# Transposes of Q and K straight from the loaded layout, weights loaded first, early filler matmuls, in a fused attention and FFN kernel

## The chip, the cores and the metric

The kernel runs on one core of a Trainium2 chip. The metric is the device time of one execution in microseconds (us). A kernel's executions lie within about 1% of one another. The profile is one execution taken by the hardware profiler. Its engines are PE (TensorE matmuls), PEld (weight loads), DVE (VectorE), ACT (ScalarE), POOL (GpSimd) and SP. Tiles whose names begin with ps lie in PSUM, the memory into which the matmuls of this kernel write. A column-half matmul is one of 64 columns that writes one of the two halves of the partitions.

## The reference

```python
# q, k, v: [8, 12, 448, 64] float32; attention with squared relu instead of softmax
scores = matmul(q, k^T) / sqrt(64)
attn   = maximum(scores, 0) ** 2 / 448
x      = matmul(attn, v)                    # -> [3584, 768]
xn     = x / sqrt(mean(x*x, -1) + 1e-6) * rms_g
g      = xn @ w_gate                        # [768, 1536]
out    = (g * sigmoid(g) * (xn @ w_val)) @ w_out
```

## The kernel before

The eight batches run as a software pipeline: while the PE computes the FFN of batch b (psG for gate, psV for value, psO for the output projection), units of the attention of batch b+1 and then its norm are merged between those matmuls. A head pair goes through these units: transposes (psT, copied to qkT by DVE), two score units of two row chunks each (psS), relu (three chunks on ACT, one on DVE), square (DVE), attend (psAV). The data type of the matmuls is bf16.

```python
def merge(main, side, head=0.0, tail=0.0):     # spreads side evenly over main by cost
    ...
    for c, f in main:
        while k < n and done >= total * (head + (1.0 - head - tail) * k / n):
            out.append(side[k][1]); k += 1
        out.append(f); done += c
...
ps_s = tile_pool("ps_s", bufs=2, PSUM)   # two banks each
ps_a = tile_pool("ps_a", bufs=1, PSUM)   # psT and psAV
ps_m = tile_pool("ps_m", bufs=3, PSUM)   # tag "mm": psG, psV, psO, psSS
...
# loads: q, k, v of batch 0, then
for s in range(NSL):                     # four slices of the gate and value weights
    load_w("g", s); load_w("v", s)
    if s == 1:
        alloc_ld(1); load("q", 1); load("k", 1)
load("v", 1); load_wo(0, 2); load_wo(1, 2)

def reorder(b, j):                       # DVE: put two heads side by side
    for nm in ("q", "k"):
        t = tpool.tile([PC, NCH, 2, D], BF16, ...)
        nc.vector.tensor_copy(out=t[:].rearrange("p c h d -> p h c d"),
            in_=ld[nm, b][:, 2*j : 2*j + 2, :].rearrange("p h (c d) -> p h c d", c=NCH))
        ldp[nm, b, j] = t

def transposes(b, j):
    if j == 0: ...; reorder(b, 0)
    if j + 1 < HP: reorder(b, j + 1)
    psT = ps_a.tile([P, 2, S], BF16, ...)
    for ti, nm in enumerate(("q", "k")):
        for c in range(NCH):
            nc.tensor.transpose(out=psT[:, ti, c*PC : (c+1)*PC],
                                in_=ldp[nm, b, j][:, c, :, :], identity=ident[:])
    ...nc.vector.tensor_copy(out=t[:], in_=psT[:])

def scores(b, j, cs):
    ...                                  # matmuls into psS
    for c, psS in zip(cs, pss):
        if on_dve: nc.vector.tensor_relu(out=r[:], in_=psS[:, :, :S])    # every fourth
        else:      nc.scalar.activation(out=r[:], in_=psS[:, :, :S], func=ACT.Relu)
        nc.vector.tensor_tensor(out=r[:], in0=r[:], in1=r[:], op=ALU.mult)

def attend(b, j):                        # two column halves of the array, 112 x 64 each
    for c in range(NCH):
        for hh in range(2):
            nc.tensor.matmul(out=psAV[hh*D : (hh+1)*D, :],
                lhsT=ld["v", b][:, 2*j + hh, c*D : (c+1)*D], rhs=rsq[b, j, c][:, hh, :], ...)
    ...
def norm(b):                             # psSS on PE, sqrt on ACT, reciprocal and six xn on DVE
    ...
for b in range(B):
    side = attention(b + 1) + [(1.1, lambda b=b: norm(b + 1))]
    ...                                  # issue the loads of batch b + 2
    for fn in merge(ffn(b), side, 0.0, 0.1): fn()
```

## Time and profile before

| | before |
|---|---|
| median of the runs beside the changed kernel | 548.75 us |
| span of the profile | 544.9 us |
| first psG starts | 51.6 us |
| idle time on the PE's timeline after that | 31 us |

The page of the kernel before: its busy table, then three rows of the span in 40 slices (tenths; PEclk is the granted clock of the PE).

```profile
PE 485.1 (89%) x3024; PEld 236.1 (43%) x3024; DVE 338.6 (62%) x586; ACT 252.3 (46%) x369; POOL 34.4 (6%) x45
...
PE   3774999879999799888999799987999899989996
...
PEclk9976999979999899999999999999999999999999
DMA  9999938150073402560054500733001200002013
```

The PE is the engine that sets the pace; only the first four slices (54 us) are far from full. The DMA engines are saturated in those and the next.

The waits of the kernel before (who waited for whom: us in total, times, longest):

```profile
DVE r L198 <- ACT r L197: 91.9, 123, 3.2
...
PE psT L163 <- DVE qp L148: 29.6, 8, 7.6
...
PE psS L182 <- ACT r L197: 7.4, 11, 1.0
PE psS L182 <- DVE r L195: 7.4, 9, 1.1
```

The PE's own waits are the last three lines. Where the first comes from is seen in the timeline of the kernel before, at the boundary between batches 2 and 3 (start us, duration us, engine, line, operation, out<-in, count, idle time before it and what ended it):

```profile
237.75 5.37 PE L286 MATMUL psO<-wo_sb,hT 128*128 128x256 bf16 x36
...
239.06 2.95 DVE L246 RECIPROCAL rstd<-rstd 128x448 f32<-128x448 f32 x1 [1.55 <-ACT rstd L243]
...
242.05 3.67 DVE L249 SCALAR_TENSOR_TENSOR xn<-xT,g_sb,rstd 128x448 bf16<-128x448 bf16 x6
...
245.63 0.29 DVE L148 COPY qp<-qb 112x512 bf16<-112x512 bf16 x1
...
245.97 0.37 PE L163 MATMUL psT<-ident,qp 112*128 112x112 bf16 x4 [2.85 <-DVE qp L148]
...
246.38 1.30 PE L260 MATMUL psG<-xn,wg_sb 128*128 128x448 bf16 x6
```

The output projection ends at 243.1 us. The PE's next instruction is a transpose of batch 4; it reads a reorder copy, which stands on DVE behind the reciprocal and six xn operations. psG waits behind the transposes, although its first xn slice is done before 243 us.

The second kind of wait, in the same batch. The DVE relu frees a psS buffer:

```profile
254.71 0.63 DVE L198 TENSOR_TENSOR r<-r 112x896 bf16<-112x896 bf16 x1 [1.38 <-ACT r L197]
254.93 0.40 PE L182 MATMUL psS<-qkT 64*112 64x448 bf16 x2
255.25 1.09 DVE L195 TENSOR_SCALAR r<-psS 112x896 bf16<-112x896 f32 x1
...
256.39 0.40 PE L182 MATMUL psS<-qkT 64*112 64x448 bf16 x2 [1.07 <-DVE r L195]
```

DVE idles 1.38 us for an ACT relu, because the square of that chunk stands first; only then comes the relu (255.25) for which the PE waits 1.07 us.

A group of eight transposes, and the matmul after it:

```profile
250.41 0.36 PE L163 MATMUL psT<-ident,qp 112*128 112x112 bf16 x4
...
250.61 0.36 PE L163 MATMUL psT<-ident,kp 112*128 112x112 bf16 x4
...
250.81 1.30 PE L260 MATMUL psV<-xn,wv_sb 128*128 128x448 bf16 x6
```

From start of the group to the next matmul it takes 0.40 us.

### The profile page before, as it was taken

What the parts mean: (1) busy time and instruction counts of PE and PEld (TensorE: products, weight loads), DVE (VectorE), ACT (ScalarE), POOL (GpSimd) and SP (SyncE); (2) the same over time, 40 slices, a digit from 0 to 9 for tenths busy, and PEclk for the clock granted to TensorE, in tenths of its full rate; (3) what the DMA queues carried; (4) which work ended last, traced back from release to release, by engine and by line L of the source; (5) the groups of instructions that cost most, each with busy time, mean ns of one, the idle gap of its engine ahead of it and who ended that gap; (6) DMA issues with size and microseconds to landing.
All of it is one profiled execution on the core that took longest, in us unless ns stands there. A gap on an engine that the chain in (4) does not pass through costs nothing.

```text
span 544.9 us, 7394 instructions
## 1 busy us (share of the span) xinstructions
PE 485.1 (89%) x3024; PEld 236.1 (43%) x3024; DVE 338.6 (62%) x586; ACT 252.3 (46%) x369; POOL 34.4 (6%) x45
## 2 busy tenths in 40 slices
PE   3774999879999799888999799987999899989996
PEld 1331444434444344444444444444445444444553
DVE  3886677467764677566774677656775677745210
ACT  2553454524545354535444454454545445553221
POOL 7330001000010001000010000100000000000000
PEclk9976999979999899999999999999999999999999
DMA  9999938150073402560054500733001200002013
GB/s 114 201 201 205 203 53 102 35 103 1 1 102 73 95 1 24 79 123 16 1 75 86 108 1 1 103 58 80 1 1 29 78 10 2 1 29 59 0 30 88
DMA packets 45858, 35.08 MB, mean 64 GB/s; under 512 B 2304, under 2 KB 42240, under 8 KB 45824
## 3 DMA queue, kind: packets, MB, share of 16 engines
q0 software_dynamic: 40560, 23.60, 31.7%
q1 hardware_dynamic: 5264, 11.02, 6.8%
q8 instruction: 23, 0.38, 0.3%
q14 instruction: 11, 0.09, 0.1%
HBM read 47.19 MB, written 11.01 MB: 107 GB/s over the span
## 4 chain that ended last, share of the span: by engine, by line
PE 73%; DVE 14%; ACT 8%; issue 2%; DMA 1%; POOL 0%; ACTq 0%; POOLq 0%
PE psV L260 20%; PE psG L260 20%; PE psO L286 14%; PE psAV L207 8%; PE psS L182 8%; DVE xn L249 5%; DVE rstd L246 4%; ACT r L197 4%; PE psT L163 3%; ACT L243 2%; DVE r L198 2%; DVE r L195 1%; ACT rstd L243 1%; DMA kb<-in_k_dram 1%; ACT xT L215 1%
## 5 line engine op out<-in xcount | busy, mean ns | idle before, releaser
L198 DVE TENSOR_TENSOR r<-r 112x896 bf16<-112x896 bf16 x192 | 119.3, 625 | 93.8 <-ACT r L197 91.9
L197 ACT ACTIVATE r<-psS 112x896 bf16<-112x896 f32 x144 | 127.0, 916 | 52.5 <-PE psS L182 52.4
L260 PE MATMUL psG<-xn,wg_sb 128*128 128x448 bf16 x576 | 129.4, 360 | 1.1 <-DVE xn L249 1.0
L260 PE MATMUL psV<-xn,wv_sb 128*128 128x448 bf16 x576 | 128.0, 359 | 0.0
L286 PE MATMUL psO<-wo_sb,hT 128*128 128x512 bf16 (+1 forms) x672 | 115.2, 326 | 0.0
L271 ACT ACTIVATE sil<-psG 128x448 bf16<-128x448 f32 x96 | 52.3, 545 | 102.2 <-PE psG L260 90.8
L277 DVE TENSOR_TENSOR hT<-sil,psV 128x448 bf16<-128x448 bf16 x96 | 59.4, 618 | 45.9 <-PE psV L260 37.8
L286 PEld LDWEIGHTS <-hT 128*128 128x128 bf16 x672 | 63.6, 98 | 49.2 <-issue 9.3
L182 PE MATMUL psS<-qkT 64*112 64x448 bf16 x384 | 64.5, 394 | 19.3 <-ACT r L197 7.4
L260 PEld LDWEIGHTS <-wg_sb 128*128 128x128 bf16 x576 | 53.0, 99 | 59.8 <-issue 19.2
L260 PEld LDWEIGHTS <-wv_sb 128*128 128x128 bf16 x576 | 52.3, 99 | 57.5 <-issue 19.2
L293 ACT COPY ost<-psO 128x512 f32<-128x512 f32 (+1 forms) x56 | 26.9, 480 | 81.4 <-PE psO L286 81.4
L195 DVE TENSOR_SCALAR r<-psS 112x896 bf16<-112x896 f32 x48 | 52.0, 1084 | 0.0
L207 PE MATMUL psAV<-r,vb 112*64 112x448 bf16 x384 | 47.7, 370 | 4.6 <-DVE qkT L169 3.8
L182 PEld LDWEIGHTS <-qkT 64*112 64x112 bf16 x384 | 21.1, 131 | 60.5 <-issue 55.2
L163 PE MATMUL psT<-ident,qp 112*128 112x112 bf16 x192 | 19.0, 226 | 29.6 <-DVE qp L148 29.6
L215 ACT ACTIVATE xT<-psAV 128x448 bf16<-128x448 f32 x48 | 26.1, 545 | 33.7 <-PE psAV L207 33.7
L163 PEld LDWEIGHTS <-qp 112*128 112x128 bf16 x192 | 14.0, 103 | 40.9 <-DVE qp L148 31.9
L207 PEld LDWEIGHTS <-vb 112*64 112x64 bf16 x384 | 19.1, 111 | 28.9 <-issue 21.4
L246 DVE RECIPROCAL rstd<-rstd 128x448 f32<-128x448 f32 x8 | 23.6, 2953 | 12.8 <-ACT rstd L243 12.8
L169 DVE COPY qkT<-psT 128x896 bf16<-128x896 bf16 x48 | 29.8, 620 | 2.3 <-PE psT L163 2.1
L249 DVE SCALAR_TENSOR_TENSOR xn<-xT,g_sb,rstd 128x448 bf16<-128x448 bf16 x48 | 29.3, 680 | 0.3
(39 smaller groups left out, 157.6 us busy)
## 6 DMA issues: line engine op xcount, KB each, us to landing
qb<-in_q_dram POOLq DMA_DIRECT2D x7, 672.0 KB, 7.3
kb<-in_k_dram POOLq DMA_DIRECT2D x7, 672.0 KB, 9.8
vb<-in_v_dram POOLq DMA_DIRECT2D x7, 672.0 KB, 8.1
out_dram<-ost SPq DMA_DIRECT2D x8, 336.0 KB, 2.8
wg_sb<-in_moe_w_gate_dram POOLq DMA_DIRECT2D x4, 576.0 KB, 20.2
wv_sb<-in_moe_w_val_dram POOLq DMA_DIRECT2D x4, 576.0 KB, 21.8
wo_sb<-in_moe_w_out_dram POOLq DMA_DIRECT2D x2, 1152.0 KB, 28.3
out_dram<-ost SPq DMA_DIRECT2D x8, 288.0 KB, 5.3
```

What stands on the lines that cost most here:

```text
L163: nc.tensor.transpose(out=psT[:, ti, c * PC : (c + 1) * PC], in_=ldp[nm, b, j][:, c, :, :], identity=ident[:],)
L182: nc.tensor.matmul(out=psS[:, hh, :S], lhsT=t[prt, 1, c * PC : (c + 1) * PC], rhs=t[prt, 0, :], start=True, stop=True,)
L195: nc.vector.tensor_relu(out=r[:], in_=psS[:, :, :S])
L197: nc.scalar.activation(out=r[:], in_=psS[:, :, :S], func=ACT.Relu)
L198: nc.vector.tensor_tensor(out=r[:], in0=r[:], in1=r[:], op=ALU.mult)
L207: nc.tensor.matmul(out=psAV[hh * D : (hh + 1) * D, :], lhsT=ld["v", b][:, 2 * j + hh, c * D : (c + 1) * D], rhs=rsq[b, j, c][:, hh, :], st ...
L246: nc.vector.reciprocal(out=rstd[:], in_=rstd[:])
L249: nc.vector.scalar_tensor_tensor(out=xn[:, kt, :], in0=xTs[b][:, kt, :], scalar=g_sb[:, kt : kt + 1], in1=rstd[:], op0=ALU.mult, op1=ALU.mult,
L260: nc.tensor.matmul(out=ps[:], lhsT=w_sb[:, kt, fb * P : (fb + 1) * P], rhs=xns[b][:, kt, :], start=(kt == 0), stop=(kt == KT - 1),)
L271: nc.scalar.activation(out=s[:], in_=psG[:], func=ACT.Silu)
L277: nc.vector.tensor_tensor(out=hTs[b // 2][:, fb, o : o + S], in0=sil[b, fb][:], in1=psV[:], op=ALU.mult)
L286: nc.tensor.matmul(out=ps[:, :w], lhsT=hTs[i][:, fk, t * P : (t + 1) * P], rhs=wo_sb[:, fk, o : o + w], start=(fk == 0), stop=(fk == FT - 1),)
```

## The change

The intent: transposes read the loaded tile directly (each head by itself, into one of the two partition halves of psT), so that no reorder copy is needed; all gate and value weights load before batch 1; dummy matmuls keep the PE busy in the first attention. The diff also does other things: squares are deferred to the next score unit (`pending`, `flush`), attend joins the second score unit, psT moves into the "mm" buffers, the side work spreads over 85% of the FFN instead of 90%, three relus of batch 0 move from DVE to ACT (48 to 45 on DVE), and some SBUF tiles get other buffer counts. (`transpose_dma` and the other layout in `load` are never used, since `PE_T = B`.)

```diff
     for s in range(NSL):
         load_w("g", s)
         load_w("v", s)
-        if s == 1:
-            alloc_ld(1)
-            load("q", 1)
-            load("k", 1)
-    load("v", 1)
+    for nm in ("q", "k", "v"):
+        load(nm, 1)
...
+    def keep_busy(n):
+        ps = ps_m.tile([P, S], FP32, name="psB", tag="mm")
+        for _ in range(n):
+            nc.tensor.matmul(out=ps[:], lhsT=ones_bf[:], rhs=busy_bf[:], start=True, stop=True)
...
-    def reorder(b, j):
-        ... (two DVE copies per head pair)
     def transposes(b, j):
-        psT = ps_a.tile([P, 2, S], BF16, name="psT", tag="ps_a")
+        psT = ps_m.tile([P, 2, S], BF16, name="psT", tag="mm")
         for ti, nm in enumerate(("q", "k")):
             for c in range(NCH):
-                nc.tensor.transpose(
-                    out=psT[:, ti, c * PC : (c + 1) * PC],
-                    in_=ldp[nm, b, j][:, c, :, :],
-                    identity=ident[:],
-                )
+                for hh in range(2):
+                    nc.tensor.transpose(
+                        out=psT[hh * D : (hh + 1) * D, ti, c * PC : (c + 1) * PC],
+                        in_=ld[nm, b][:, 2 * j + hh, c * D : (c + 1) * D],
+                        identity=ident[:],
+                    )
...  (in scores)
-            nc.vector.tensor_tensor(out=r[:], in0=r[:], in1=r[:], op=ALU.mult)
+            squares.append(
+                lambda r=r, eng=eng: eng.tensor_tensor(out=r[:], in0=r[:], in1=r[:], op=ALU.mult)
+            )
+        flush()
+        pending.extend(squares)
...  (in attention)
+            if b == 0:
+                add(0.3, lambda: keep_busy(2))
+            add(1.2, lambda j=j: scores(b, j, (2, 3)), lambda j=j: j and attend(b, j - 1))
+            if b == 0:
+                add(0.3, lambda: keep_busy(2))
...
+    keep_busy(16)
     for fn in merge([], attention(0) + [(1.1, lambda: norm(0))]):
...
-        for fn in merge(ffn(b), side, 0.0, 0.1):
+        for fn in merge(main, side, 0.0, 0.15):
```

More of the change, by code (lines that the diff above doesn't have):

```diff
@@ L66 @@
     ldpool = ctx.enter_context(tc.tile_pool(name="ld", bufs=2))
-    tpool = ctx.enter_context(tc.tile_pool(name="tsb", bufs=2))
+    qtpool = ctx.enter_context(tc.tile_pool(name="qkT", bufs=2))
     apool = ctx.enter_context(tc.tile_pool(name="attn", bufs=10))
-    xpool = ctx.enter_context(tc.tile_pool(name="xT", bufs=2))
+    xpool = ctx.enter_context(tc.tile_pool(name="xT", bufs=1))
     npool = ctx.enter_context(tc.tile_pool(name="norm", bufs=2))
@@ L76, with new_qkT, transpose_dma @@
     ps_m = ctx.enter_context(tc.tile_pool(name="ps_m", bufs=3, space=bass.MemoryType.PSUM))
-    def head_rows(t, b, h0, h1):
-        return t[b, h0:h1].rearrange("h (p c) d -> p h (c d)", c=NCH)
     ld = {}
-    def alloc_ld(b):
-        for nm in ("q", "k", "v"):
-            ld[nm, b] = ldpool.tile([PC, H, NCH * D], BF16, name=nm + "b", tag=nm + "b")
+    qkT = {}
+    src_of = {"q": q, "k": k, "v": v}
+    PE_T = B
     def load(nm, b, h0=0, h1=H):
-        src = {"q": q, "k": k, "v": v}[nm]
-        nc.gpsimd.dma_start(out=ld[nm, b][:, h0:h1, :], in_=head_rows(src, b, h0, h1))
+        runs = nm == "v" or b < PE_T
+        if (nm, b) not in ld:
+            shape = [PC, H, NCH * D] if runs else [PC, NCH, H * D]
+            ld[nm, b] = ldpool.tile(shape, BF16, name=nm + "b", tag=nm + "b")
+        t = ld[nm, b]
+        src = src_of[nm][b, h0:h1]
+        if runs:
+            nc.gpsimd.dma_start(out=t[:, h0:h1, :], in_=src.rearrange("h (p c) d -> p h (c d)", c=NCH))
+        else:
+            nc.gpsimd.dma_start(
+                out=t[:].rearrange("p c (h d) -> p c h d", d=D)[:, :, h0:h1, :],
+                in_=src.rearrange("h (p c) d -> p c h d", c=NCH),
+            )
+    def new_qkT(b):
+        qkT[b] = qtpool.tile([P, HP, 2, S], BF16, name="qkT", tag="qkT")
+    def transpose_dma(b):
+        new_qkT(b)
+        for ti, nm in enumerate(("q", "k")):
+            for c in range(NCH):
+                nc.sync.dma_start_transpose(
+                    out=qkT[b][:, :, ti, c * PC : (c + 1) * PC], in_=ld[nm, b][:, c, :]
+                )
     wg_sb = wpool.tile([P, KT, F], BF16, name="wg_sb", tag="wg")
@@ L110, in load_wo @@
         )
-    alloc_ld(0)
+    ones_bf = const.tile([P, P], BF16, name="ones_bf", tag="ones_bf")
+    nc.vector.memset(ones_bf[:], 1.0)
+    busy_bf = const.tile([P, S], BF16, name="busy_bf", tag="busy_bf")
+    nc.vector.memset(busy_bf[:], 0.0)
+    def keep_busy(n):
+        ps = ps_m.tile([P, S], FP32, name="psB", tag="mm")
+        for _ in range(n):
+            nc.tensor.matmul(out=ps[:], lhsT=ones_bf[:], rhs=busy_bf[:], start=True, stop=True)
     load("q", 0, 0, 2)
@@ L116 @@
     masks.make_identity(nc, ident[:])
-    ones_bf = const.tile([P, P], BF16, name="ones_bf", tag="ones_bf")
-    nc.vector.memset(ones_bf[:], 1.0)
     eps_col = const.tile([P, 1], FP32, name="eps_col", tag="eps_col")
@@ L141, with relu_on, square_on, flush @@
     xTs = {}
-    qkT = {}
-    ldp = {}
-    def reorder(b, j):
-        for nm in ("q", "k"):
-            t = tpool.tile([PC, NCH, 2, D], BF16, name=nm + "p", tag=nm + "p")
-            nc.vector.tensor_copy(
-                out=t[:].rearrange("p c h d -> p h c d"),
-                in_=ld[nm, b][:, 2 * j : 2 * j + 2, :].rearrange("p h (c d) -> p h c d", c=NCH),
-            )
-            ldp[nm, b, j] = t
     def transposes(b, j):
         if j == 0:
-            xTs[b] = xpool.tile([P, KT, S], BF16, name="xT", tag="xT")
-            reorder(b, 0)
-        if j + 1 < HP:
-            reorder(b, j + 1)
-        psT = ps_a.tile([P, 2, S], BF16, name="psT", tag="ps_a")
+            new_qkT(b)
+        psT = ps_m.tile([P, 2, S], BF16, name="psT", tag="mm")
         for ti, nm in enumerate(("q", "k")):
             for c in range(NCH):
-                nc.tensor.transpose(
-                    out=psT[:, ti, c * PC : (c + 1) * PC],
-                    in_=ldp[nm, b, j][:, c, :, :],
-                    identity=ident[:],
-                )
-        t = tpool.tile([P, 2, S], BF16, name="qkT", tag="qkT")
-        nc.vector.tensor_copy(out=t[:], in_=psT[:])
-        qkT[b, j] = t
-    rsq = {}
-    state = {"n": 0}
+                for hh in range(2):
[3 more added lines that the diff above has]
+                        identity=ident[:],
+                    )
+        nc.vector.tensor_copy(out=qkT[b][:, j, :, :], in_=psT[:])
+    rsq = {}
+    pending = []
+    def relu_on(b, j, c):
+        return "dve" if c == 3 and (b or j % 2) else "act"
+    def square_on(b, j, c):
+        return "dve"
+    def flush():
+        while pending:
+            pending.pop(0)()
     def scores(b, j, cs):
-        t = qkT[b, j]
         pss = []
@@ L183, in scores @@
                     out=psS[:, hh, :S],
-                    lhsT=t[prt, 1, c * PC : (c + 1) * PC],
-                    rhs=t[prt, 0, :],
+                    lhsT=qkT[b][prt, j, 1, c * PC : (c + 1) * PC],
+                    rhs=qkT[b][prt, j, 0, :],
                     start=True,
@@ L189, in scores @@
             pss.append(psS)
+        squares = []
         for c, psS in zip(cs, pss):
             r = apool.tile([PC, 2, S], BF16, name="r", tag="r")
-            on_dve = state["n"] % 4 == 3
-            state["n"] += 1
-            if on_dve:
+            if relu_on(b, j, c) == "dve":
                 nc.vector.tensor_relu(out=r[:], in_=psS[:, :, :S])
@@ L197, in scores @@
                 nc.scalar.activation(out=r[:], in_=psS[:, :, :S], func=ACT.Relu)
-            nc.vector.tensor_tensor(out=r[:], in0=r[:], in1=r[:], op=ALU.mult)
+            eng = nc.gpsimd if square_on(b, j, c) == "pool" else nc.vector
+            squares.append(
+                lambda r=r, eng=eng: eng.tensor_tensor(out=r[:], in0=r[:], in1=r[:], op=ALU.mult)
+            )
             rsq[b, j, c] = r
+        flush()
+        pending.extend(squares)
     x2s = {}
@@ L213, in attend, with add @@
                 )
+        if j == 0:
+            xTs[b] = xpool.tile([P, KT, S], BF16, name="xT", tag="xT")
+            x2s[b] = npool.tile([P, KT, S], BF16, name="x2", tag="x2", bufs=1)
         xT = xTs[b]
         nc.scalar.mul(out=xT[:, j, :], in_=psAV[:], mul=inv_attn)
-        if j == 0:
-            x2s[b] = npool.tile([P, KT, S], BF16, name="x2", tag="x2")
-        nc.vector.tensor_tensor(out=x2s[b][:, j, :], in0=xT[:, j, :], in1=xT[:, j, :], op=ALU.mult)
-    def attention(b):
-        units = [(0.4, lambda: transposes(b, 0))]
-        for j in range(HP):
-            units.append((0.5, lambda j=j: scores(b, j, (0, 1))))
-            if j + 1 < HP:
-                units.append((0.4, lambda j=j: transposes(b, j + 1)))
-            units.append((0.5, lambda j=j: scores(b, j, (2, 3))))
-            if j:
-                units.append((0.8, lambda j=j: attend(b, j - 1)))
-        units.append((0.8, lambda: attend(b, HP - 1)))
+        pending.append(
+            lambda: nc.vector.tensor_tensor(
+                out=x2s[b][:, j, :], in0=xT[:, j, :], in1=xT[:, j, :], op=ALU.mult
+            )
+        )
+    def attention(b):
+        units = []
+        def add(cost, *fns):
+            units.append((cost, lambda: [f() for f in fns]))
+        if b < PE_T:
+            add(0.4, lambda: transposes(b, 0))
+        for j in range(HP):
+            add(0.5, lambda j=j: scores(b, j, (0, 1)))
+            if b < PE_T and j + 1 < HP:
+                add(0.4, lambda j=j: transposes(b, j + 1))
+            if b == 0:
[3 more added lines that the diff above has]
+                add(0.3, lambda: keep_busy(2))
+        add(0.1, flush)
+        add(0.8, lambda: attend(b, HP - 1), flush)
         return units
@@ L321 @@
             side = attention(b + 1) + [(1.1, lambda b=b: norm(b + 1))]
+        main = ffn(b)
         if b + 2 < B:
-            alloc_ld(b + 2)
             for nm in ("q", "k", "v"):
                 load(nm, b + 2)
-        for fn in merge(ffn(b), side, 0.0, 0.1):
+            at = len(main) * 2 // 3
+            main[at:at] = [(0, lambda b=b: b + 2 < PE_T or transpose_dma(b + 2))]
+        for fn in merge(main, side, 0.0, 0.15):
             fn()
```

## The prediction

> **What bounds it now.** TensorE is busy 89% of the 544.9 us span (page, busy table), VectorE 62%, ScalarE 46%. From 51 us on, where the FFN of batch 0 runs, the PE's timeline has only 31 us of idle time:
> - *Norm boundaries.* "PE psT waits for DVE qp" is 29.6 us in 8 waits (waits): one of 7.6 us before FFN 0, six of 2.86 us. There the timeline shows sqrt, reciprocal 2.95 us, six xn 3.67 us, then the next batch's reorder copies, and only then the transposes, which stand before the first psG on the PE. The last boundary, without transposes, shows psG starting on the first xn slice and stalling 0.25 us per slice. After the first two boundaries the granted clock halves (psG 2.24, not 1.14 us).
> - *psS waits*, 7.4 us for ACT relu and 7.4 for DVE relu: about 1 us per batch, where the DVE relu stands behind a square that waits for ACT, and 1.4 us per even batch, where eight score matmuls follow one another.
> - *Start*: 51.6 us before the first psG, DVE 87% busy, about 5.2 us per head pair.
>
> **Removed.** 96 reorder copies (28 us DVE) and the boundary transposes' wait for them; squares no longer hold up the DVE relu; psT and psAV no longer share one bank.
>
> **Added.** 16 instead of 8 transposes per head pair. Eight take 0.39 us now (49 ns apart). The new form (112 rows, 64 columns, two column halves) has psAV's shape, whose halves start 2-4 ns apart in the trace, 189 ns per pair. The Trainium skill (TensorE: Matmul & The Clock Gate, Packing small matmuls) says that column tiles run concurrently; the trace agrees for psAV. So I estimate 0.4-0.5 us per head pair: +2 us. If they don't overlap, 0.8 us: +14 us. Keep-busy matmuls lie in waiting time. psT now takes one of three "mm" buffers; I allow 2 us of stalls.
>
> **Moved.** q and k of batch 1 now load after all gate and value weights. The queue delivers 0.2 MB/us; the 8.16 MB up to k1 have landed at 46.6 us in the old trace. Attention 0 gets shorter (about 4.2 us per pair, norm done near 43 us), but the next stage begins with batch 1's transposes. So it starts at about 46.7, not 50.9 us, DMA-bound.
>
> **On the critical path.** Start -4. Boundaries: transposes run in the gap and psG follows xn slice by slice, -1.6 us after even FFNs; after odd ones the norm also comes one output unit (2.7 us) earlier, -2.5; with the avoided half clock -4 at the first, -3.5 at the second; sum about -15; the last unchanged. DVE relu waits -7; the last head pair's waits move from even to odd batches, about 0. Transposes +2, buffers +2. Net about -22.
>
> **Predicted: 526 us**, 80% range 517 to 537. Chances: faster by over 2% 0.84, within 2% 0.13, slower 0.03.
>
> **What would show it.** No PE wait for DVE over about 1 us at boundaries; transposes of the two halves starting within a few ns, psT groups about 0.45 us; first psG near 47-48 us, after a PE wait ended by DMA of k1; psS waits for the DVE relu nearly gone; DVE busy about 30 us less; psG and psV unchanged at 1.14 us.
>
> **What would make it wrong.** Column-half transposes that serialize (near 538); psT in the "mm" pool making psG or psV wait for late DVE copies at every head pair; attention 0 slower than 46 us; a longer half-clock period after the start's wait.

## The result, and the profile after

The changed kernel takes 521.07 us in the median (520.45 to 522.97), the kernel before 548.75 us beside it. The ratio is 0.949, 95% interval 0.944 to 0.955: faster. (A ratio here is the mean time of one kernel's runs over that of the other's of the same rounds, so not quite the ratio of the medians.) The span of the profiled run is 518.7 us.

The page of the changed kernel, the same rows as before:

```profile
PE 485.5 (94%) x3429; PEld 234.3 (45%) x3448; DVE 306.2 (59%) x488; ACT 251.5 (48%) x372; POOL 34.4 (7%) x45
...
PE   7953999999989999999998999999998999999996
...
PEclk9995999999999999999999999999999999999998
DMA  9999984820087100860047500860001300011013
```

DVE lost 32 us, 28 of them the removed copies. The PE is busy as long as before in a shorter span. What is left of its idle time is mostly in the third and fourth slice.

The waits of the changed kernel:

```profile
PE psS L199 <- ACT r L213: 7.1, 17, 1.0
...
PE psG L295 <- DVE xn L284: 4.0, 17, 0.2
```

The wait of psS for the DVE relu is gone from the list, and that of psT for DVE too. The boundary between batches 2 and 3 in the timeline of the changed kernel:

```profile
222.05 5.37 PE L321 MATMUL psO<-wo_sb,hT 128*128 128x256 bf16 x35
...
226.66 3.67 DVE L284 SCALAR_TENSOR_TENSOR xn<-xT,g_sb,rstd 128x448 bf16<-128x448 bf16 x6
227.35 0.39 PE L173 MATMUL psT<-ident,qb 112*64 112x112 bf16 x8
...
227.57 0.36 PE L173 MATMUL psT<-ident,kb 112*64 112x112 bf16 x8
...
227.87 0.55 PE L295 MATMUL psG<-xn,wg_sb 128*128 128x448 bf16 x2
...
228.60 0.35 PE L295 MATMUL psG<-xn,wg_sb 128*128 128x448 bf16 x1 [0.18 <-DVE xn L284]
```

The transposes follow the output projection at once, and psG follows the xn slices with stalls of about 0.2 us each.

A group of transposes in the middle of a batch, in the timeline of the changed kernel:

```profile
174.99 0.39 PE L173 MATMUL psT<-ident,qb 112*64 112x112 bf16 x8
...
175.22 0.36 PE L173 MATMUL psT<-ident,kb 112*64 112x112 bf16 x8
...
175.51 1.31 PE L295 MATMUL psV<-xn,wv_sb 128*128 128x448 bf16 x6
```

It takes 0.52 us to the next matmul, not 0.40.

The start, PE alone:

```profile
33.68 1.47 PE L273 MATMUL psSS<-x_276,ones_bf 128*128 128x448 bf16 x6
44.97 0.58 PE L173 MATMUL psT<-ident,qb 112*64 112x112 bf16 x8 [9.82 <-DMA qb<-in_q_dram]
48.45 0.59 PE L173 MATMUL psT<-ident,kb 112*64 112x112 bf16 x8 [2.89 <-DMA kb<-in_k_dram]
48.97 1.30 PE L295 MATMUL psG<-xn,wg_sb 128*128 128x448 bf16 x3
```

Attention 0 is done 7.3 us sooner than before (psSS at 33.7 instead of 41.0 us), but the PE then idles 12.7 us for q and k of batch 1, which now stand in the DMA queue behind all the gate and value weights. The first psG gains only 2.6 us.

To see where the rest came from, I added up the distances from the start of each matmul to the start of the next, by the pair of tiles, from the first psG of batch 0 to the first psG of batch 7. Every microsecond of that stretch is in exactly one row (worked out from the records of the traces):

| step on the PE, us in total | before | changed |
|---|---|---|
| psO to psT (boundary) | 18.8 | 1.2 |
| psS to psS (scores, with their waits) | 36.4 | 26.9 |
| psG to psG | 82.7 | 85.7 |
| psV to psV | 82.3 | 80.2 |
| 41 groups of transposes: within, out of, and (except at boundaries) into them | 23.3 | 31.1 |
| all other steps | 200.0 | 194.7 |
| sum | 443.4 | 419.7 |

So 17.6 us came from the boundaries, of which 3.0 went back inside psG (stalls for xn slices, less the half clock after the first two boundaries, which fell away); 9.5 us from waits for relu; and the transposes themselves got 7.8 us dearer.

### The profile page after: what moved, and what is told of

Same layout as the page of the kernel before. It is cut to its first block, busy times and chain, and to the rows that moved or that the text cites. A ratio compares the mean times of both kernels' runs of the same rounds, so it can differ in the third digit from the quotient of the medians.

```text
span 518.7 us, 8176 instructions
## 1 busy us (share of the span) xinstructions
PE 485.5 (94%) x3429; PEld 234.3 (45%) x3448; DVE 306.2 (59%) x488; ACT 251.5 (48%) x372; POOL 34.4 (7%) x45
## 2 busy tenths in 40 slices
DMA packets 45863, 35.14 MB, mean 68 GB/s; under 512 B 2305, under 2 KB 42241, under 8 KB 45825
## 3 DMA queue, kind: packets, MB, share of 16 engines
q0 software_dynamic: 40560, 23.60, 33.3%
## 4 chain that ended last, share of the span: by engine, by line
PE 79%; DMA 8%; DVE 5%; ACT 5%; POOL 1%; issue 1%; POOLq 0%
PE psG L295 22%; PE psV L295 21%; PE psO L321 17%; PE psS L199 7%; PE psAV L228 7%; DMA kb<-in_k_dram 5%; PE psT L173 4%; DMA wv_sb<-in_moe_w_val_dram 3%; DVE xn L284 3%; DVE rstd L281 2%; ACT r L213 2%; ACT L278 1%; ACT ost L328 1%; PE psSS L273 1%; ACT rstd L278 0%
## 5 line engine op out<-in xcount | busy, mean ns | idle before, releaser
L295 PE MATMUL psV<-xn,wv_sb 128*128 128x448 bf16 x576 | 125.4, 354 | 0.0
L321 PE MATMUL psO<-wo_sb,hT 128*128 128x256 bf16 (+1 forms) x653 | 111.4, 324 | 1.2 <-issue 0.5
L216 DVE TENSOR_TENSOR r<-r 112x896 bf16<-112x896 bf16 x192 | 109.5, 618 | 0.3 <-ACT r L213 0.3
L295 PEld LDWEIGHTS <-wg_sb 128*128 128x128 bf16 x576 | 51.3, 98 | 61.0 <-issue 19.1
L211 DVE TENSOR_SCALAR r<-psS 112x896 bf16<-112x896 f32 x45 | 49.1, 1091 | 42.5 <-PE psS L199 42.5
L199 PE MATMUL psS<-qkT 64*112 64x448 bf16 x384 | 59.0, 372 | 7.8 <-ACT r L213 7.1
L228 PE MATMUL psAV<-r,vb 112*64 112x448 bf16 x384 | 46.0, 359 | 1.3 <-DVE r L216 0.8
L199 PEld LDWEIGHTS <-qkT 64*112 64x112 bf16 x384 | 19.0, 124 | 46.3 <-issue 43.3
L239 ACT ACTIVATE xT<-psAV 128x448 bf16<-128x448 f32 x48 | 26.1, 544 | 12.3 <-PE psAV L228 10.3
L173 PE MATMUL psT<-ident,qb 112*64 112x112 bf16 x384 | 18.8, 220 | 9.8 <-DMA qb<-in_q_dram 9.8
L93 POOL DMA_DIRECT2D qb<-in_q_dram x10 | 8.9, 886 | 227.1 <-PE psT L173 221.5
```

The costliest lines, as they stand in the source:

```text
L173: nc.tensor.transpose(out=psT[hh * D : (hh + 1) * D, ti, c * PC : (c + 1) * PC], in_=ld[nm, b][:, 2 * j + hh, c * D : (c + 1) * D], identi ...
L199: nc.tensor.matmul(out=psS[:, hh, :S], lhsT=qkT[b][prt, j, 1, c * PC : (c + 1) * PC], rhs=qkT[b][prt, j, 0, :], start=True, stop=True,)
L216: lambda r=r, eng=eng: eng.tensor_tensor(out=r[:], in0=r[:], in1=r[:], op=ALU.mult)
L228: nc.tensor.matmul(out=psAV[hh * D : (hh + 1) * D, :], lhsT=ld["v", b][:, 2 * j + hh, c * D : (c + 1) * D], rhs=rsq[b, j, c][:, hh, :], st ...
L295: nc.tensor.matmul(out=ps[:], lhsT=w_sb[:, kt, fb * P : (fb + 1) * P], rhs=xns[b][:, kt, :], start=(kt == 0), stop=(kt == KT - 1),)
L321: nc.tensor.matmul(out=ps[:, :w], lhsT=hTs[i][:, fk, t * P : (t + 1) * P], rhs=wo_sb[:, fk, o : o + w], start=(fk == 0), stop=(fk == FT - 1),)
```

## The experiments

All kernels below gave correct results and were timed in three rounds beside the kernel before (medians of that 547.8 to 548.7 us). They fall into three sets, each run on another chip of the same kind; between sets, a difference as small as that of these medians (0.9 us) says nothing.

| kernel | median us | ratio to before |
|---|---|---|
| changed | 521.07 | 0.949 |
| x1_order | 515.71 | 0.941 |
| x2_nobusy | 521.80 | 0.952 |
| x3_inline | 532.93 | 0.972 |
| x4_reorder | 521.64 | 0.952 |
| x5_wide | 513.85 | 0.937 |
| x6_serial | 521.50 | 0.951 |
| x7_ta | 524.89 | 0.959 |
| x8_order_nobusy | 514.66 | 0.940 |
| x10_tail | 519.80 | 0.948 |
| x11_split | 524.94 | 0.957 |
| y1_order_wide | 506.75 | 0.923 |
| y2_filler | 506.29 | 0.923 |

### Is the start bound by the load order?

```diff
     for s in range(NSL):
         load_w("g", s)
         load_w("v", s)
-    for nm in ("q", "k", "v"):
-        load(nm, 1)
+        if s == 1:
+            load("q", 1)
+            load("k", 1)
+    load("v", 1)
```

> The changed kernel with q and k of batch 1 loaded where the kernel before had them (after two of four weight slices). Theory: the start of the changed kernel is bound by the DMA of k of batch 1 (landed 48.4 us, the PE idle for 12.7 us before it), which now lands near 35 us; the first psG moves from 49.0 to about 40 us and the whole gets 8 to 11 us shorter, 510 to 513 us. Rival: the weights that now land later (last slices near 46 us instead of 40) hold FFN 0 up instead, or attention 0 does: under 3 us gained.

It was 515.71 us (runs from 513.25 to 517.70), 5.4 us less than the changed kernel (the spans differ by 6.4: 512.3 and 518.7). The PE at the start of x1_order:

```profile
35.98 0.39 PE L175 MATMUL psT<-ident,kb 112*64 112x112 bf16 x8 [0.58 <-DMA kb<-in_k_dram]
40.05 3.42 PE L297 MATMUL psG<-xn,wg_sb 128*128 128x448 bf16 x6 [3.68 <-DVE xn L286]
```

The mechanism is as expected: the first psG starts at 40.05 instead of 48.97 us, and the norm of batch 0, no longer a DMA, is what it waits for. The size was missed: 2.5 us come back in the next stage (first psG of batch 0 to that of batch 1: 60.8 instead of 58.3 us), where psG now waits for the xn slices and runs at the half clock that begins as the 3.7 us of idle PE end (40.1 to 46.9 us by the clock's records; psV matmuls follow each other at 373 ns there and at 189 ns afterwards). The changed kernel has 2.6 us of half clock in that stage, from 49.0 to 51.5 us. So "all weights first" alone costs the changed kernel about 5 us.

### Are the keep-busy matmuls worth anything?

```diff
-    keep_busy(16)
...
-            if b == 0:
-                add(0.3, lambda: keep_busy(2))     # both places
```

> The changed kernel without any keep-busy matmul. Theory: worth nothing here, since the PE waits for the DMA of k of batch 1 in any case: psSS of batch 0 may come later (33.7 us now), the first psG stays at 49 us, the whole within 1.5 us of 521. Rival: the warm clock in attention 0 is worth time: slower by 4 us or more.

> The kernel with the old load order (x1_order) without keep-busy matmuls. Without them psSS of batch 0 came at 33.0 instead of 33.7 us while the start was still bound by DMA; now the start ends with the norm of batch 0. Theory: the keep-busy matmuls are still worth nothing: within 1.5 us of x1_order, psSS near 33 us. Rival: a warm PE matters once DMA doesn't bind: 3 us or more slower.

Without them the changed kernel takes 521.80 us, and x1_order 514.66 instead of 515.71 us: no difference in either case. psSS of batch 0 comes at 33.0 and 33.6 us without them, at 33.7 and 33.6 with them. The attention of batch 0 is not bound by the PE, and its clock does not matter.

### The deferred squares

```diff
-            squares.append(
-                lambda r=r, eng=eng: eng.tensor_tensor(out=r[:], in0=r[:], in1=r[:], op=ALU.mult)
-            )
+            eng.tensor_tensor(out=r[:], in0=r[:], in1=r[:], op=ALU.mult)
```

> The changed kernel with each square issued right after its relu, as before. Theory: the DVE relu stands again behind a square that waits for ACT, the roughly 1 us PE stall per batch on psS comes back: 5 to 8 us slower, 526 to 529 us, with waits of psS for the DVE relu of about 7 us in all. Rival: the longer spacing of the score units already hides it: within 2 us.

It was 532.93 us, 11.9 us slower than the changed kernel, more than expected. The waits of x3_inline show the old pattern again:

```profile
DVE r L215 <- ACT r L213: 87.9, 91, 2.5
...
PE psS L199 <- DVE r L211: 5.8, 6, 1.0
```

In the step table, psS to psS goes from 26.9 back to 37.2 us, about the value before the change (36.4); the list of waits shows only part of this, since it counts a wait from the modelled end of a pipelined matmul. The other 2.7 us of the stretch are spread over small differences in other rows. This is the largest effect of any single part, and it is not in the intent of the change as described.

### What are the new transposes worth?

First the copies and full-width transposes back in (and the qkT buffer single, for room):

```diff
+    def reorder(b, j):  ... as in the kernel before ...
     def transposes(b, j):
         if j == 0:
             new_qkT(b)
+            reorder(b, 0)
+        if j + 1 < HP:
+            reorder(b, j + 1)
...
-                for hh in range(2):
-                    nc.tensor.transpose(out=psT[hh*D : (hh+1)*D, ...], in_=ld[nm, b][:, 2*j + hh, c*D : (c+1)*D], ...)
+                nc.tensor.transpose(out=psT[:, ...], in_=ldp[nm, b, j][:, c, :, :], ...)
```

> The changed kernel with the transposes of before: reorder copies on DVE, then eight full-width transposes per head pair (qkT in one buffer instead of two, for room). Theory: a group of column-half transposes costs 215 ns more PE time than a full-width one in the traces, because the PE loses about 93 ns when it goes from a full-width to a column-half matmul and again on the way back; so this saves about 7.7 us in the PE-bound stages and loses about 6 us at the boundaries, where the transposes wait for copies behind xn: within 3 us of the changed kernel. Rival: reading straight from the loaded layout is what made the change fast: 8 us or more slower.

It was 521.64 us, the same as the changed kernel. So the rewrite of the transposes, in this schedule, is worth nothing in sum. The boundary of x4_reorder after an even batch has its wait back:

```profile
230.55 0.29 DVE L172 COPY qp<-qb 112x512 bf16<-112x512 bf16 x1
...
230.90 0.37 PE L187 MATMUL psT<-ident,qp 112*128 112x112 bf16 x4 [3.17 <-DVE qp L172]
...
231.31 1.30 PE L309 MATMUL psG<-xn,wg_sb 128*128 128x448 bf16 x6
```

In the step table psO to psT rises from 1.2 to 12.2 us, psG to psG falls from 85.7 to 81.4 (no more stalls for slices of xn), and the groups of transposes fall from 31.1 to 22.9 us. The gain at the boundary and the dearer transposes cancel. Of the 12.2 us, the three boundaries after even FFNs take 3.44 us each, and those after odd FFNs, where the 85% puts the norm one output unit earlier, 0.64 us each although the copies are back. Attention 0 is longer too, by the copies or the single qkT buffer (psSS at 35.8 instead of 33.7 us); the wait for k of batch 1 hides that here.

Why are they dearer? In the trace of the changed kernel the two halves of a pair start 2 to 4 ns apart, and pairs follow each other at 49 ns (the second at about 70), as eight full-width ones did. But the last FFN matmul before a group starts 282 ns before it instead of 189, and the last transpose is followed by the next FFN matmul after 145 ns instead of 49. That is 93 ns on the way in and 96 on the way out. About the same, 279 to 283 ns, stands before psS and psAV in both kernels. The Trainium skill says in "TensorEngine Tiling (Array Packing)", Key Properties, that changing the tiling mode drains the TensorE; it names no time, and I had not looked there when I predicted. What the PE does in that time the runs do not settle: the weight load of the group's first transpose is recorded at 174.99 us, together with its own matmul and 281 ns after the last psG matmul began (174.71), whereas in the kernel before it begins 2 ns after that matmul (both at 250.22). So the weight load, 0.1 us long in both traces, is not overlapped at the change of form, and that alone is about as long as the loss; no run separates it from a drain. Two ways to avoid the change of form were tried. One loads the two heads of a pair side by side, so that full-width transposes need no copy:

```diff
-        runs = nm == "v" or b < PE_T
+        runs = nm == "v" or b < 2          # else tile [PC, NCH, H*D], DMA runs of 64 elements
...
             for c in range(NCH):
+                if b >= 2:
+                    nc.tensor.transpose(
+                        out=psT[:, ti, c * PC : (c + 1) * PC],
+                        in_=ld[nm, b][:, c, 2 * j * D : (2 * j + 2) * D],
+                        identity=ident[:],
+                    )
+                    continue
                 for hh in range(2):
```

> The changed kernel with q and k of batches 2 to 7 loaded with the two heads of a pair side by side (runs of 64 elements in the DMA instead of 256), so that eight full-width transposes per head pair read them without a copy. Theory: 36 groups lose 215 ns each: 6 to 8 us faster than the changed kernel, 513 to 515 us; the DMA takes longer but has time to spare. Rival: the shorter DMA runs make loads late, or the switch cost isn't real: same or slower.

It was 513.85 us, 7.2 us less than the changed kernel, as expected. A group of transposes in its timeline:

```profile
174.37 0.36 PE L174 MATMUL psT<-ident,qb 112*128 112x112 bf16 x4
174.57 0.36 PE L174 MATMUL psT<-ident,kb 112*128 112x112 bf16 x4
174.76 1.30 PE L303 MATMUL psV<-xn,wv_sb 128*128 128x448 bf16 x6
```

It is 0.39 us to the next matmul again; the groups sum to 23.9 us. The price is in the DMA: packets under 512 bytes go from 2305 to 66816, the software queue's share of the DMA engines from 33.3% to 49.4%, and a load of k lands after 11.6 instead of 9.8 us. The queue has time to spare after the start, so this costs nothing.

The other way puts the transposes next to psAV, which has the same form:

```diff
             if b < PE_T and j + 1 < HP:
-                add(0.4, lambda j=j: transposes(b, j + 1))
+                add(0.4)
...
-            add(1.2, lambda j=j: scores(b, j, (2, 3)), lambda j=j: j and attend(b, j - 1))
+            add(1.2, lambda j=j: scores(b, j, (2, 3)), lambda j=j: j and attend(b, j - 1),
+                lambda j=j: j + 1 < HP and transposes(b, j + 1))
```

> The changed kernel with the transposes of the next head pair issued right after psAV, which has the same column-half form, in place of between FFN matmuls. Theory: one way into and one way out of the column-half form fall away for 35 groups, 187 ns each: about 6 us faster, 514 to 516 us, if psS doesn't wait for the later qkT copy. Rival: the 93 ns is not a change of form but something each group pays: within 1.5 us.

It was 524.89 us, 3.8 us slower: a miss. The change of form was in fact saved. The step from psAV to psT takes 186 ns, with nothing added to psAV's own 189 ns. But the condition that I had named failed, as the timeline of x7_ta shows:

```profile
181.09 0.61 DVE L178 COPY qkT<-psT 128x896 bf16<-128x896 bf16 x1
...
181.76 0.59 PE L199 MATMUL psS<-qkT 64*112 64x448 bf16 x4 [1.03 <-DVE qkT L178]
```

The copy of qkT now stands on DVE behind the relu and squares of the same unit, and psS waits for it 27 times, 12.6 us in all. The attention of batch 0 is stretched too (psSS at 39.4 us), but there the DMA hides it.

Last, does the overlap of the halves depend on their alternating?

```diff
-            for c in range(NCH):
-                for hh in range(2):
+            for hh in range(2):
+                for c in range(NCH):
```

> The changed kernel with the four transposes of the first column half issued before the four of the second, so that neighbours fall into the same half. Theory: the halves overlap only when they alternate; a group of 16 takes about 0.9 us instead of 0.52, 42 groups lie in PE-bound stages: 13 to 17 us slower, 534 to 538 us. Rival: the array overlaps them in any order, or the 0.52 us is not set by the overlap: within 3 us.

It was 521.50 us, no slower; my theory fell. The group in its timeline:

```profile
174.90 0.40 PE L173 MATMUL psT<-ident,qb 112*64 112x112 bf16 x8
175.12 0.39 PE L173 MATMUL psT<-ident,kb 112*64 112x112 bf16 x8
175.44 0.74 PE L295 MATMUL psV<-xn,wv_sb 128*128 128x448 bf16 x3
```

A group takes 543 ns to the next matmul, 26 ns more than with alternating halves. Sixteen in single file at 49 ns would be 784 ns. After the first pair the starts fall into two interleaved rows, in each mostly 49 ns apart (the two 13 to 30 ns from each other), so two transposes are in work at any time although the program puts four of one half in front. The records do not say which half each belongs to: either the later half went ahead, or two of the same half overlap. No run separates these.

### The rest of the schedule

```diff
-        for fn in merge(main, side, 0.0, 0.15):
+        for fn in merge(main, side, 0.0, 0.1):
```

> The changed kernel with the attention of the next batch spread over 90% of the FFN, as before, instead of 85%. The merge then puts the norm of even batches in the same slot, and that of odd FFNs one output unit (2.7 us) later. Theory: the earlier norm is what closes the boundary after odd FFNs; with the later one psG follows xn slice by slice there too (about 1.5 us of stalls at 3 boundaries), while the two score units of the last head pair no longer follow one another in odd FFNs (1.4 us of waits less): within 2.5 us of 521, with stalls of psG for xn at all boundaries. Rival: the 85% is worth a good part of the gain: 5 us or more slower.

It was 519.80 us, within what was expected: the wider tail brings nothing. With the late norm psG to psG rises from 85.7 to 89.3 us, and psS to psS falls from 26.9 to 20.0 us, as score units no longer crowd at the end of odd FFNs.

```diff
-            add(1.2, lambda j=j: scores(b, j, (2, 3)), lambda j=j: j and attend(b, j - 1))
+            add(0.5, lambda j=j: scores(b, j, (2, 3)))
+            if j:
+                add(0.8, lambda j=j: attend(b, j - 1))
```

> The changed kernel with psAV again as a unit of its own among the FFN matmuls, not right after the scores of chunks 2 and 3. The merge leaves the norm in the same slots. Theory: 35 head pairs pay one more way in and out of the column-half form, about 0.09 us net each: 3 us slower, 523 to 525 us. Rival: the change of form is not what costs, or the finer spacing helps as much: within 1 us, or faster.

It was 524.94 us, 3.9 us slower, as the change of form has it: each extra visit among FFN matmuls pays its way in and out.

### A version that beats both

y1_order_wide is the edits of x1_order and x5_wide together. y2_filler is that without the keep-busy matmuls in attention 0, and with 18 of them where x1_order's PE really goes idle:

```diff
-    keep_busy(16)              # and both keep_busy(2) in attention
...
         main = ffn(b)
+        if b == 0:
+            main.insert(0, (0, lambda: keep_busy(18)))
```

> Old load order and the wide layout of q and k for batches 2 to 7 together. Theory: the two gains lie in different stages and add: 5.5 us at the start and 7.2 us in the PE-bound stages, 507 to 510 us. Rival: once the start is shorter the loads of batch 2 with their short runs come late: over 511 us.

> As y1_order_wide, without the keep-busy matmuls in attention 0, and with 18 of them between the first transposes of batch 1 and the first psG, where x1_order has the PE idle for 3.7 us and then 6.8 us of halved clock. Theory: keeping the PE busy pays only there: the stage of FFN 0 goes from 60.8 to about 58.5 us, 2 to 2.5 us off y1_order_wide. Rival: the slices of psG that wait for xn let the clock drop all the same: no difference.

y1_order_wide took 506.75 us, ratio 0.923 (0.921 to 0.926) to the kernel before: the two gains add. y2_filler took 506.29 us, no difference. Its FFN 0 stage did get shorter, from 60.6 to 56.8 us, more than expected. But k of batch 1 landed at 38.0 us in this run, after 2.0 us of waiting, and the fillers behind it took 5.1 us and not 3.4 (18 times 189 ns): the clock was halved from 39.1 to 42.5 us. So the first psG came at 43.4 instead of 40.2 us, which ate the gain. Whether fewer fillers would have won something was not tried.

## Why the prediction was right or wrong

The time, 521.07 us, lies in the range of 517 to 537 us, 5 us under the point; the direction had 0.84. That it lies so near is in part luck: the transposes cost more than predicted, and the relu and attend parts gained more, and these errors partly cancel. Point by point:

- *Boundaries, -15 us: right, with one wrong step.* psO to psT fell by 17.6 us and 3.0 came back as stalls in psG; the half clock at the first two boundaries is gone, as expected. The step "after odd ones the norm also comes one output unit earlier, -2.5" did not bring a gain of the kernel: x10_tail took it back and was no slower, since the crowded score units cost as much.
- *DVE relu waits, -7 us: right mechanism, too small.* psS to psS fell by 9.5 us, and undoing the deferral alone cost 11.9 us (10.3 of it in psS to psS). I had read the size off the list of waits, which misses what lies within the modelled end of a matmul.
- *Transposes, +2 us: mis-sized.* The overlap and the 49 ns per pair were as predicted, but the sum was +7.8 us: the term left out the change of the array's form, 93 ns in and 96 out. x4_reorder shows that this cancels the rewrite's gain at the boundaries; x5_wide took the term away and won 7.2 us.
- *Buffers, +2 us: not seen.* No wait of psG or psV for a copy of psT stands in the list.
- *Start, -4 us: right mechanism.* It was -2.6, DMA-bound as said; k of batch 1 landed at 48.4, not 46.6 us. The 1.8 us were a misreading: in the old trace too, the last load of the same set (the fourth slice of the value weights, issued at 24.1 us) landed only at 48.2 us. At 46.6 us the queue had moved 8.16 MB in both traces, but not all of them were of that set. Also, DVE is busy 87% only from 13.6 to 27.2 us of the start, and 71% of the whole 51.6 us.
- *Keep-busy matmuls lie in waiting time: right* (x2_nobusy, x8_order_nobusy).
- *Not predicted:* joining attend to the scores, 3.9 us by x11_split. By size, that and the larger relu term account for the total coming out better in spite of the dearer transposes.

The single undoings do not add up to the whole 27.7 us. Deferral and joining give 15.8, and the load order costs about 5. Much of the rest is boundary time that more than one part can close by itself: after odd FFNs the direct transposes close it with the late norm (x10_tail), and the early norm with the copies (x4_reorder, psO to psT 6.5 us below the kernel before). Another part is attention 0, whose psSS comes at 37.6 us in x3_inline and 35.8 in x4_reorder instead of 33.7: both were made where the wait for k of batch 1 hides this. The move of psT out of psAV's bank was not undone by itself.

## What to carry to other kernels

Count the changes of array form in a tuned PE stream, not only the columns: here a small column-half group between full-width matmuls cost its two switches (0.19 us), which a layout that permits full-width operands avoided. When an engine works in order, issue the operation that frees a buffer for the bottleneck ahead of work that waits for another engine. Before ordering loads, look at which one the first instruction of the next stage needs; here a faster stage in front of it only turned into idle time.

## What the Trainium skill lacked or had wrong

- "TensorEngine Tiling (Array Packing)", Key Properties, says that changing the tiling mode drains the TensorE, but not how much it costs. Here it was 93 ns on the way in and 96 on the way out between full-width and column-half matmuls (282 instead of 189 ns before, 145 instead of 49 ns after a group), and nothing between psAV and transposes of the same form (186 ns). "TensorE: Matmul & The Clock Gate", Packing small matmuls, recommends column tiles without naming this cost.
- "TensorE: Matmul & The Clock Gate", Packing small matmuls, says that matmuls are "strict FIFO, no reordering". x6_serial leaves this open: sixteen transposes with four of one half in front of four of the other took 543 ns, against 517 when alternating and 784 ns in single file, with starts in two interleaved rows. Either a column half's matmuls do not wait for those of the other half ahead of them in the program, or two of the same half overlap; the first would contradict the page, and the records do not name the halves.
- The same page, in its table of goals, warns of PE-idle gaps over about 3 us. The traces agree in the main: the 3.7 us of idle PE in x1_order end in 6.8 us of half clock. But a half clock sometimes came with a shorter gap: in y2_filler the clock was halved for 3.4 us, from 1.1 us after the end of a wait of 2.0 us; and of the six boundary waits of 2.85 us in the kernel before, the first two went with a half clock (114.6 to 121.4 and 182.9 to 186.3 us) and the others did not. The page does not say that fillers bring nothing where the stage does not wait for the PE: 40 of them in attention 0 were worth nothing (521.80 without and 521.07 us with them).
